# First loads of a gated state-space and feed-forward kernel cut smaller, reordered and spread over other queues

## The chip, the cores and the metric

One core of a Trainium2 chip runs the whole program. The metric is device time in microseconds, the median of several runs. The profile comes from one further execution. Its times start at the beginning of the span that the profile covers.

## The reference

For each of 2048 rows of x (448 wide) the reference mixes two branches with one gate:

```python
g = sigmoid((x * gate_w).sum(-1, keepdims=True))
a = ssm(x)                          # complex linear recurrence over the rows, then a projection, plus x * Dskip
b = silu(x @ w1) @ w2               # w1: 448 x 1792, w2: 1792 x 448
return g * a + (1 - g) * b
```

The recurrence is `h = Lam_bar * h + Bu[t]`, with `Lam_bar = exp(exp(log_dt) * (Lambda_re + 1j * Lambda_im))`. The three vectors `log_dt`, `Lambda_re` and `Lambda_im` (448 values each) are called the parameter rows below.

## The kernel before

**Tiling.** Rows 2k and 2k+1 of x sit side by side, so x is 1024 x 896: the left half holds the even rows, the right half the odd ones. Each half is worked on in two blocks of 512. Matmuls need x transposed (tile XT), with its 448 columns split into blocks j = 0, 1, 2 of 128 and a remainder of 64 (j = 3). W1 (tile W1E) is split in the same way along its rows, and along its 1792 columns into 14 blocks of 128. The columns 0 to 767 (six blocks, `NF1`) are used first.

**Who orders the work.** Every engine's order is written out by hand. A helper (`Tracker`) records each operation with the tiles it reads and writes, and puts a semaphore wait ahead of an operation where one is needed; an engine runs its list strictly in that order. A load is recorded at L226 and a transposing load at L229, whatever tile it fills. Loads issued by SyncE (SP) go to one DMA queue, loads issued by ScalarE (ACT) to another.

**The opening.** TensorE cannot start on data before x and W1 arrive, so it first runs `NWARM` = 20 matmuls on constants (L486). Then, in TensorE's order:

- `turn_k` (L494) transposes 128 x 128 pieces of x on TensorE (L496), k = 0..3 for each j; `turned_x` (L504) lets VectorE (DVE) copy them from PSUM into XT (L507).
- `ffn1_first` (L433) is a generator that issues the 24 matmuls of the first block of rows (L439): for j = 0 twelve of 256 columns (two halves h of the rows times six W1 blocks, `c0` blocks first, then `c1`), for j = 1 and j = 2 six of 512 columns each. It stops at the places listed at L444, and the main program puts other work there.
- `rd` (L470) is a DVE copy inside tile R that needs all three parameter rows; `mm_cols` (L473, matmuls at L477) turns R into columns, and DVE copies them out as PV (L527). PV feeds a chain of small ACT and DVE operations (exp, phases) from L561 on.
- `ffn1_rem` (L448, matmuls at L452) adds the remainder j = 3 to six blocks.
- All later matmuls of the first product and of the input projection go through `lanes` (L366, matmuls at L371).

**The loads before the change** (L287 to L303), each pair on SP and ACT at once: x columns 0 to 127 (two pieces of 64 KB, `ld_x`), W1 rows of j = 0 (two pieces of 96 KB, `ld_w`), x columns 128 to 383 (two of 128 KB), W1 of j = 1 (two of 96 KB, `ld_wh`), the three parameter rows (`ld_row`; two on SP, one on ACT), W1 of j = 2 (two of 96 KB), x columns 384 to 511 (two of 64 KB). Then SP and ACT share the rest of W1: the remainder rows for the first columns (keys W1Er, 48 KB each), columns 768 to 1279 (W1Ed, 256 and 128 KB), the remainder rows for the later columns (W1Es, 64 KB each) and columns 1280 to 1791 (W1Ee, 128 and 256 KB). SP then waits for W1Er (L314) and issues transposing loads of the other rows of x and of B_re and B_im.

**GpSimd (POOL)** meanwhile builds an identity matrix (L330, L331), a ramp IOTA (L334, L336) and a few zeros (L338); it issues no load.

Of the kernel before, what the change touches and what calls it, by code (L numbers as in the profile page):

```python
# [8 lines left out]
AF = mybir.ActivationFunctionType  # L9
# [11 lines left out]
F_FF = 1792  # L21
# [1 line left out]
NK = 1024  # L23
NKT = 8
NF1 = 6
NWARM = 20


class Dma:
# [121 lines left out]
def gated_mix(nc, A_x, A_Lambda_re, A_Lambda_im, A_B_re, A_B_im, A_C_re, A_C_im, A_log_dt,  # L151
              A_Dskip, B_x, B_w1, B_w2, gate_w, out):
    with ExitStack() as ctx:
        E = ctx.enter_context
        T = Tracker(nc, ctx)

        def sb(name, shape, dtype):
            return E(nc.sbuf_tensor(name, list(shape), dtype))
# [5 lines left out]
        W1E = sb("W1E", [128, 4, F_FF], BF16)  # L164
# [16 lines left out]
        JK = sb("JK", [128, 2], BF16)  # L181
# [7 lines left out]
        ID = sb("ID", [128, 128], BF16)  # L189
# [5 lines left out]
        HP = sb("HP", [128, 1], F32)  # L195
# [25 lines left out]
        ps = E(nc.psum_tensor("ps", [128, 8, 512], F32))  # L221
# [3 lines left out]
        def ld(eng, dst, src, key, group=None):  # L225
            return T.dma(eng, lambda e: e.dma_start(dst, src), writes=[key], group=group)  # L226
# [23 lines left out]
        def row(v):  # L250
            return v.rearrange("(o n) -> o n", o=1)

        XH = XN[:, 0:8 * D].rearrange("p (k c) -> p k c", k=4)
        XA = [f"XA{n}{i}" for n in range(3) for i in range(2)]
        FA, FB = 768, 1280
        x0 = x2[0:512, 0:512].rearrange("(k p) c -> p k c", p=128)

        def ld_w(eng, j, f0=0, f1=FA, key=""):
            ld(eng, W1E[:, j, f0:f1], B_w1[j * 128:(j + 1) * 128, f0:f1], f"W1Ej{j}{key}")

        def ld_row(eng, i, v):
            ld(eng, R[i:i + 1, 0:D], row(v), f"R{i}", gR if i < 2 else gR2)

        def ld_w3(eng, j0, j1, f0, f1, key):
            ld(eng, W1E[:, j0:j1, f0:f1], B_w1[j0 * 128:j1 * 128, f0:f1].rearrange("(j p) f -> p j f", p=128),
               f"W1E{key}{j0}")

        def ld_wr(eng, c, later):
            p = slice(64 * c, 64 * c + 64)
            if later:  # L270
                return ld(eng, W1E[p, 3, 384:896].rearrange("p (n f) -> p n f", n=2),
                          B_w1[384:448, FA:].rearrange("p (n c f) -> p n c f", n=2, c=2)[:, :, c, :], f"W1Es{c}")
            return ld(eng, W1E[p, 3, 0:384], B_w1[384:448, 384 * c:384 * c + 384], f"W1Er{c}")

        HALVES = ((0, "sp"), (1, "act"))

        def ld_x(n, c0, c1):
            for i, eng in HALVES:
                k = slice(2 * i, 2 * i + 2)
                ld(eng, XH[:, k, c0:c1], x0[:, k, c0:c1], f"XA{n}{i}")  # L280

        def ld_wh(j):
            for i, eng in HALVES:
                ld(eng, W1E[64 * i:64 * i + 64, j, 0:FA], B_w1[j * 128 + 64 * i:j * 128 + 64 * i + 64, 0:FA],
                   f"W1Ej{j}{i}")

        ld_x(0, 0, 128)  # L287
        for c, eng in HALVES:
            ld_w(eng, 0, 384 * c, 384 * c + 384, c)
        ld_x(1, 128, 384)  # L290
        ld_wh(1)
        for i, (eng, v) in enumerate((("sp", A_log_dt), ("sp", A_Lambda_re), ("act", A_Lambda_im))):
            ld_row(eng, i, v)
        ld_wh(2)
        ld_x(2, 384, 512)
        T.op("act", lambda e: e.activation(JK[:, 0:1], HP[:, :], AF.Exp), reads=["HP"], writes=["JK0"])
        gE = [ld_wr(eng, c, False) for c, eng in enumerate(("sp", "act"))]
        ld_w3("sp", 0, 2, FA, FB, "d")
        ld_w3("act", 2, 3, FA, FB, "d")
        for c, eng in enumerate(("sp", "act")):  # L300
            ld_wr(eng, c, True)
        ld_w3("sp", 0, 1, FB, F_FF, "e")
        ld_w3("act", 1, 3, FB, F_FF, "e")  # L303
        BTK = [f"BT{i}" for i in range(4)] + ["BTz"]
        gBT = T.group()
        def ld_b(dst, src, key):
# [12 lines left out]
        for i, src in enumerate((A_B_re, A_B_im)):  # L319
# [11 lines left out]
        T.op("pool", lambda e: e.affine_select(  # L331
            out=ID[:, :], in_=ID[:, :], pattern=[[-1, 128]], compare_op=ALU.is_equal, fill=0.0,
            base=0, channel_multiplier=1), reads=["ID"], writes=["ID"])
        T.op("pool", lambda e: e.iota(IOTA[:, :].bitcast(I32), pattern=[[1, NK]], base=0, channel_multiplier=0),  # L334
             writes=["IOTA"])
        T.op("pool", lambda e: e.tensor_copy(IOTA[:, :], IOTA[:, :].bitcast(I32)), reads=["IOTA"], writes=["IOTA"])  # L336
# [8 lines left out]
        def nxt():  # L345
            n_bank[0] += 1
            return BANKS[(n_bank[0] - 1) % len(BANKS)]
# [61 lines left out]

        def wj(fb):  # L410
            i, c = fb // 2, fb % 2
            return [f"W1Ej{j}{c}" for j in range(3) for c in range(2)] if i < 3 else ["W1Ed0", "W1Ed2"] if i < 5 else ["W1Ee0", "W1Ee1"]

        def w1(fb):
            return lambda p, j: W1E[p, j, ff(fb) * 128:(ff(fb) + 1) * 128] if j < 3 else \
# [17 lines left out]
        def ffn1_first():  # L433
            banks = [nxt() for _ in range(NF1)]
            for j, h in ((0, 0), (0, 1), (1, None), (2, None)):
                c = slice(0, 512) if h is None else slice(256 * h, 256 * h + 256)
                for n, fb in enumerate((0, 2, 4, 1, 3, 5)):
                    bank = banks[fb]
                    T.op("pe", lambda pe, fb=fb, bank=bank, j=j, h=h, c=c: pe.matmul(  # L439
                        ps[:, bank, c], W1E[:, j, ff(fb) * 128:(ff(fb) + 1) * 128], XT[:, j, c],  # L440
                        start=(h == 0), stop=(h == 0), skip_group_check=(h != 0)),
                        reads=[f"W1Ej{j}{i}" for i in (range(2) if j else (fb % 2,))] + [f"XTe0{j}" if h is None else f"XTe0{j}{h}"],
                        writes=[f"ps{bank}"])
                    if (j, h, n) in ((0, 1, 2), (0, 1, 5), (1, None, 2), (1, None, 5)):  # L444
                        yield
            yield banks

# [34 lines left out]
        def warm(n, b):  # L482
            def mm(pe):
                ins = None
                for _ in range(n):
                    ins = pe.matmul(ps[:, b, 0:128], ones, ones, start=True, stop=True)  # L486
                return ins
            T.op("pe", mm, writes=[f"ps{b}"])

        warm(NWARM, 5)  # L490
        PB = (6, 6, 7, 6)
        xp = [ps[:, b, 0:256].bitcast(BF16) for b in PB]

        def turn_k(j, k, b=None):  # L494
            b = PB[j] if b is None else b
            T.op("pe", lambda pe: pe.transpose(  # L496
                ps[:, b, 0:256].bitcast(BF16)[:, k * 128:(k + 1) * 128], XH[:, k, j * 128:(j + 1) * 128], ID[:, :]),
                reads=[f"XA{(j + 1) // 2}{k // 2}", "ID"], writes=[f"ps{b}"])

        def turn_x(j, i):  # L500
            for k in (2 * i, 2 * i + 1):
                turn_k(j, k)

        def turned_x(j, i=None, b=None):  # L504
            c, key = (slice(0, 512), f"XTe0{j}") if i is None else (slice(256 * i, 256 * i + 256), f"XTe0{j}{i}")
            b = PB[j] if b is None else b
            T.op("dve", lambda e: e.tensor_copy(XT[:, j, c], ps[:, b, 0:256].bitcast(BF16)[:, c]),  # L507
                 reads=[f"ps{b}"], writes=[key])

        for i in range(2):  # L510
            for k in (2 * i, 2 * i + 1):
                turn_k(0, k, 6 + i)
            turned_x(0, i, 6 + i)
        warm(4, 4)
        first = ffn1_first()
        next(first)
        for i in range(2):
            turn_x(1, i)
        turned_x(1)
        next(first)  # L520
        for i in range(2):
            turn_x(2, i)
        turned_x(2)
        rd()
        next(first)
        T.op("pe", mm_cols, reads=["R0", "R1", "R2", "Rd", "ID"], writes=["pv"])
        T.op("dve", lambda e: e.tensor_copy(  # L527
            PV[:, :, :], ps[:, 7, 256:288].rearrange("p (t c) -> p t c", c=8)[:, :, 0:4]),
            reads=["pv", "ps7"], writes=["PV"])
        next(first)  # L530
        for i in range(2):
            turn_x(3, i)

        names = {}

# [5 lines left out]
        def col(n):  # L541
            i = pc(n)
            return P[:, i, :]
# [13 lines left out]
        def pact(o, a, f, ra, scale=1.0, bias=0.0):  # L557
            T.op("act", lambda e: e.activation(col(o), a, f, bias=bias, scale=scale),
                 reads=ra, writes=[o])
# [3 lines left out]
            col("phf"), LIM, 1.0 / TWO_PI, col("dt"), ALU.mult, ALU.mult), reads=["PV", "dt"], writes=["phf"])  # L563
        ptt("ar", col("dt"), LRE, ALU.mult, ["dt", "PV"])
        pact("mag", col("ar"), AF.Exp, ["ar"])
        turned_x(3)
        T.op("dve", lambda e: e.tensor_copy(XR[64:128, 0:512], xp[3][0:64, :]), reads=["ps6"], writes=["XR0a"])
        T.op("act", lambda e: e.activation(JK[:, 0:1], HP[:, :], AF.Silu), reads=["HP"], writes=["JK0"])
        ld_b(GWB, gate_w, "GW")
        ld_b(DB, A_Dskip, "DB")  # L570
        pts("phr", col("phf"), MAGIC, -MAGIC, ALU.add, ALU.add, ["phf"])
# [8 lines left out]
            reads=["f2"] + SGN, writes=["f2s"])  # L580
        first = next(first)
# [54 lines left out]
        def xblock(b):  # L636
            v = XN[:, 4 * b * D:4 * (b + 1) * D].rearrange("p (k c) -> p k c", k=4) if b > 1 else \
                XH[:, :, b * D:(b + 1) * D]
            return v, [*(XA if b < 2 else []), *([f"XN{b // 2}"] if b else [])]

# [24 lines left out]
        for n in (32, 64):  # L665
            T.op("dve", lambda e, n=n: e.tensor_copy(GD[n:2 * n, :, :], GD[0:n, :, :]), reads=["GW", "DB"],
                 writes=["GW", "DB"])
# [7 lines left out]
             writes=["BTz"] + BTK[2:4])  # L675
# [486 lines left out]
        f = ffn1(2)  # L1162
# [100 lines left out]
```

## Time and profile before

| | us |
|---|---|
| median of 3 runs (lowest, highest) | 137.19 (136.63, 137.26) |
| time of the profiled execution | 136.76 |
| its span | 135.2 |
| around the span | 1.56 |
| TensorE busy | 131.8 |
| first matmul on data (L439) | at 4.36 |
| first matmul of `lanes` (L371) | at 10.21 |

The chain of waits lists, in order of time, the pieces of work that led to the last instruction: start, length, what. The timeline lists instructions engine by engine: start, length, engine, line, operation, tile written and tile read, how often. "SPq" and "ACTq" are DMA issues: the length is the time that the issuing queue was held, not the transfer. The view of DMA issues gives KB and the time from issue to landing.

### The profile page before, as it was taken

To read this page: it belongs to the slowest core of one execution; us is meant where nothing else is said; L and a number is where in the kernel's file an instruction comes from. 1 tells how busy PE (TensorE), PEld (TensorE's weight loads), DVE (VectorE), ACT (ScalarE), POOL (GpSimd) and SP (SyncE) were. 2 spreads that over 40 slices of the span, in tenths; PEclk is the share of its full clock that TensorE was granted. 3 is DMA by queue.
4 is the path that set the end of the run, shared out by engine and by line. 5 is a ranking of instruction groups with operands and counts; after the bars stand their busy time and mean duration, and the time that the engine had idled before them with its cause. 6 is when DMAs were issued, how large, how long until landed. Compare 5 with 4: busy or idle time off the path is not lost.

```text
span 135.2 us, 2635 instructions
## 1 busy us (share of the span) xinstructions
PE 131.8 (98%) x1075; PEld 67.3 (50%) x1075; DVE 115.1 (85%) x151; ACT 93.6 (69%) x146; POOL 15.9 (12%) x32
## 2 busy tenths in 40 slices
PE   7899999999999999999999999999999999999993
PEld 7644555554444554444445544445555555555552
DVE  1469999917899798999999999999999999994554
ACT  0459798899939999769999597797114437879200
POOL 7108349550000000000000000000000000000000
PEclk9999999999999999999999999999999999999999
DMA  3889959997996310000222000000000000222123
GB/s 94 244 239 248 184 102 249 175 371 195 263 179 108 70 47 0 0 0 0 60 48 52 5 0 0 0 5 0 0 0 0 0 0 11 95 92 78 68 80 124
DMA packets 25280, 11.78 MB, mean 87 GB/s; under 512 B 17651, under 2 KB 24758, under 8 KB 25270
## 3 DMA queue, kind: packets, MB, share of 16 engines
q1 hardware_dynamic: 23268, 10.47, 32.4%
q10 hardware_dynamic: 2002, 1.17, 3.0%
q8 instruction: 8, 0.13, 0.4%
q14 instruction: 2, 0.02, 0.0%
HBM read 5.34 MB, written 1.84 MB: 53 GB/s over the span
## 4 chain that ended last, share of the span: by engine, by line
PE 95%; DMA 2%; DVE 1%; SPq 0%; issue 0%
PE ps L371 44%; PE ps L795 16%; PE ps L810 16%; PE ps L1048 15%; PE ps L439 3%; DMA W1E<-in_B_w_dram 2%; DVE TMPS L1072 1%; PE ps L496 1%; PE ps L452 1%; SPq L226 0%; PE ps L477 0%
## 5 line engine op out<-in xcount | busy, mean ns | idle before, releaser
L371 PE MATMUL ps<-XT,W1E 64*128 64x512 bf16 x325 | 41.5, 376 | 0.0
L460 ACT ACTIVATE AT<-ps 128x1024 bf16<-128x1024 f32 x28 | 28.2, 1018 | 7.3 <-PE ps L371 7.2
L371 PEld LDWEIGHTS ps<-XT,W1E 64*128 64x128 bf16 x325 | 17.7, 94 | 18.1 <-issue 0.4
L371 PE MATMUL ps<-XT,BT 64*128 64x512 bf16 x156 | 22.5, 376 | 0.0
L810 PE MATMUL ps<-W,AT 64*128 64x448 bf16 x224 | 21.5, 349 | 0.0
L795 PE MATMUL ps<-W,AT 128*128 128x448 bf16 x112 | 21.4, 353 | 0.0
L795 PEld LDWEIGHTS ps<-W,AT 128*128 128x128 bf16 x112 | 10.9, 98 | 10.5 <-issue 0.4
L810 PEld LDWEIGHTS ps<-W,AT 64*128 64x128 bf16 x224 | 10.9, 94 | 10.4
L839 ACT ACTIVATE BT<-ps,GT 128x448 bf16<-128x448 f32 x8 | 5.1, 634 | 13.2 <-PE ps L795 13.2
L895 DVE SCALAR_TENSOR_TENSOR HS<-VE,P,ps 128x512 bf16<-128x512 bf16 (+1 forms) x13 | 9.6, 780 | 3.9 <-PE ps L371 3.9
L371 PEld LDWEIGHTS ps<-XT,BT 64*128 64x128 bf16 x156 | 8.5, 94 | 8.9 <-DVE HS L895 0.3
L939 DVE TENSOR_TENSOR_SCAN G<-P,Q 128x1024 f32<-128x1024 f32 (+1 forms) x6 | 11.4, 1922 | 0.0
L1048 PE MATMUL ps<-CO,VE 128*128 128x448 bf16 (+2 forms) x63 | 11.1, 332 | 0.0
L1048 PE MATMUL ps<-CO,HS 128*128 128x448 bf16 x56 | 11.1, 352 | 0.0
L371 PE MATMUL ps<-XR,W1E 64*128 64x512 bf16 x25 | 9.2, 376 | 0.0
L1048 PEld LDWEIGHTS ps<-CO,VE 128*128 128x128 bf16 x63 | 6.0, 98 | 4.8
L1048 PEld LDWEIGHTS ps<-CO,HS 128*128 128x128 bf16 x56 | 5.5, 98 | 5.1
L892 DVE TENSOR_TENSOR Q<-G,COS 128x2048 bf16<-128x2048 f32 (+1 forms) x4 | 7.0, 1756 | 0.1
L892 DVE TENSOR_TENSOR Q<-G,SIN 128x2048 bf16<-128x2048 f32 (+1 forms) x4 | 7.0, 1751 | 0.0
L857 ACT ACTIVATE VE<-ps 128x1024 bf16<-128x1024 f32 x6 | 6.1, 1020 | 1.2 <-PE ps L371 1.2
L859 ACT ACTIVATE ps<-VE,P 128x1024 f32<-128x1024 bf16 x6 | 6.7, 1118 | 0.2
L895 DVE SCALAR_TENSOR_TENSOR VE<-HS,P,FP 128x512 bf16<-128x512 bf16 (+1 forms) x7 | 6.6, 977 | 0.1
(123 smaller groups left out, 180.7 us busy)
## 6 DMA issues: line engine op xcount, KB each, us to landing
W<-in_B_w_dram SPq DMA_DIRECT2D x2, 784.0 KB, 6.4
XN<-in_A_x_dram SPq DMA_DIRECT2D x1, 896.0 KB, 5.4
out_dram<-OT SPq DMA_DIRECT2D x8, 112.0 KB, 1.7
out_dram<-TMPS SPq DMA_DIRECT2D x7, 112.0 KB, 1.7
HS<-HS SPq DMA_DIRECT2D x4, 128.0 KB, 2.4
XN<-in_A_x_dram SPq DMA_DIRECT2D x1, 384.0 KB, 3.5
W1E<-in_B_w_dram SPq DMA_DIRECT2D x3, 96.0 KB, 3.0
W1E<-in_B_w_dram ACTq DMA_DIRECT2D x3, 96.0 KB, 3.2
```

The lines of the kernel that those rows point to most:

```text
L371: ins = pe.matmul(ps[:, bank, :], w(p, j), xh(odd, h, j, p), start=start and j == js[0], stop=stop and j == js[-1], skip_group_check=seeded)
L439: T.op("pe", lambda pe, fb=fb, bank=bank, j=j, h=h, c=c: pe.matmul(ps[:, bank, c], W1E[:, j, ff(fb) * 128:(ff(fb) + 1) * 128], XT[:, j, c] ...
L460: T.op("act", lambda e: e.activation(a[:, fb:fb + n, :], ps[:, bank:bank + n, :], AF.Silu), reads=[f"ps{bank + i}" for i in range(n)], wri ...
L795: ins = pe.matmul(ps[:, bank, 0:D], a[:, fb, q * 128:(q + 1) * 128], W2[:, ff(fb), :], start=(first and fb == 0), stop=(fb == NFB - 1), sk ...
L810: ins = pe.matmul(ps[:, bank, 0:D], a[p, fb, q * 128:(q + 1) * 128], W2[p, ff(fb), :], start=(start and fb == 0), stop=(not start and fb = ...
L839: T.op("act", lambda e: e.activation(bs(tile), ps[:, bank, 0:D], AF.Copy, scale=sc), reads=[f"ps{bank}", "GT2" if h else "GRI"], writes=ks)
L857: T.op("act", lambda e: e.activation(VE[:, m:m + 2, hs], ps[:, b[0]:b[0] + 2, :], AF.Copy), reads=[f"ps{i}" for i in b], writes=vs)
L859: T.op("act", lambda e: e.activation(ps[:, o[0]:o[0] + 2, :], VE[:, m:m + 2, hs], AF.Copy, scale=c1("lr", pt)), reads=vs + ["lr"], writes= ...
L892: T.op("dve", lambda e: e.tensor_tensor(o, a, b, op), reads=reads, writes=writes)
L895: T.op("dve", lambda e: e.scalar_tensor_tensor(o, a, s, b, ALU.mult, ALU.add), reads=reads, writes=writes)
L939: T.op("dve", lambda e: e.tensor_tensor_scan(G[:, c, w], rb, Q1[:, c, w], init, ALU.mult, ALU.add), reads=[f"Q1{c}", "rr", f"G{c}"], write ...
L1048: ins = pe.matmul(ps[:, bank, c], state(kt, odd, m), CO[:, m, c], start=False, stop=(m == YB[-1]), skip_group_check=True)
```

## The change

- `NWARM` falls from 20 to 16.
- x columns 0 to 127 come in four pieces of 32 KB instead of two of 64 KB, and W1 of j = 0 in four pieces of 48 KB (64 rows by 384 columns) instead of two of 96 KB, in turn.
- x columns 128 to 255 (two of 64 KB) come ahead of W1 of j = 1; x columns 256 to 511 (two of 128 KB) behind it.
- ACT issues only the first seven loads. W1 of j = 2 is one piece of 192 KB on SP, and SP issues all the rest of W1, sixteen loads in all ahead of its first transposing load.
- The three parameter rows are issued by POOL, behind the identity matrix and ahead of IOTA. In the program each is 16 pieces of 28 values; before, each was one piece of 448.
- TensorE's order: the second pair of transposes of j = 0 comes behind the first three matmuls; `mm_cols` comes behind the last matmuls of j = 0 and ahead of those of j = 1 (before: between the two halves of j = 1); the transposes of j = 2 and j = 3 come behind the first and second half of the matmuls of j = 1.
- DVE's order: `rd` and the copy to PV come ahead of the copies of j = 2; the two small operations `phf` and `ar`, which wait for ACT, too.

```diff
-NWARM = 20
+NWARM = 16
...
+        def ld_k(k):
+            for i, eng in HALVES:
+                ld(eng, XH[:, k + i, 0:128], x0[:, k + i, 0:128], f"XA0{k + i}")
+
...
-        def ld_wh(j):
+        def ld_wh(j, f0, f1, key=""):
             for i, eng in HALVES:
-                ld(eng, W1E[64 * i:64 * i + 64, j, 0:FA], B_w1[j * 128 + 64 * i:j * 128 + 64 * i + 64, 0:FA],
-                   f"W1Ej{j}{i}")
-
-        ld_x(0, 0, 128)
-        for c, eng in HALVES:
-            ld_w(eng, 0, 384 * c, 384 * c + 384, c)
-        ld_x(1, 128, 384)
-        ld_wh(1)
-        for i, (eng, v) in enumerate((("sp", A_log_dt), ("sp", A_Lambda_re), ("act", A_Lambda_im))):
-            ld_row(eng, i, v)
-        ld_wh(2)
-        ld_x(2, 384, 512)
+                ld(eng, W1E[64 * i:64 * i + 64, j, f0:f1], B_w1[j * 128 + 64 * i:j * 128 + 64 * i + 64, f0:f1],
+                   f"W1Ej{j}{key}{i}")
+
+        for c in range(2):
+            ld_k(2 * c)
+            ld_wh(0, 384 * c, 384 * c + 384, c)
+        ld_x(1, 128, 256)
+        ld_wh(1, 0, FA)
+        ld_x(2, 256, 512)
         T.op("act", lambda e: e.activation(JK[:, 0:1], HP[:, :], AF.Exp), reads=["HP"], writes=["JK0"])
-        gE = [ld_wr(eng, c, False) for c, eng in enumerate(("sp", "act"))]
+        ld_w("sp", 2)
+        gE = [ld_wr("sp", c, False) for c in range(2)]
...
+        for i, v in enumerate((A_log_dt, A_Lambda_re, A_Lambda_im)):
+            ld_row("pool", i, v)
...
-                    if (j, h, n) in ((0, 1, 2), (0, 1, 5), (1, None, 2), (1, None, 5)):
+                    if (j, h, n) in ((0, 0, 2), (0, 1, 2), (0, 1, 5), (1, None, 2), (1, None, 5)):
                         yield
...
-        for i in range(2):
+        def turn_0(i):
             for k in (2 * i, 2 * i + 1):
                 turn_k(0, k, 6 + i)
             turned_x(0, i, 6 + i)
+
+        def turn_all(j):
+            for i in range(2):
+                turn_x(j, i)
+
+        turn_0(0)
         warm(4, 4)
         first = ffn1_first()
         next(first)
-        for i in range(2):
-            turn_x(1, i)
+        turn_0(1)
+        next(first)
+        turn_all(1)
         turned_x(1)
-        next(first)
-        for i in range(2):
-            turn_x(2, i)
-        turned_x(2)
         rd()
         next(first)
...
-        next(first)
-        for i in range(2):
-            turn_x(3, i)
...
+        next(first)
+        turn_all(2)
+        turned_x(2)
+        next(first)
+        turn_all(3)
         turned_x(3)
```

The remaining W1 loads (`ld_w3`, `ld_wr`) change only from `"act"` to `"sp"`, and the lists of keys follow the new pieces.

More of the change, by code (lines that the diff above doesn't have):

```diff
@@ L253, in gated_mix @@
         XH = XN[:, 0:8 * D].rearrange("p (k c) -> p k c", k=4)
-        XA = [f"XA{n}{i}" for n in range(3) for i in range(2)]
+        XA = [f"XA0{k}" for k in range(4)] + [f"XA{n}{i}" for n in (1, 2) for i in range(2)]
         FA, FB = 768, 1280
@@ L280, in ld_x @@
                 ld(eng, XH[:, k, c0:c1], x0[:, k, c0:c1], f"XA{n}{i}")
-        def ld_wh(j):
+        def ld_wh(j, f0, f1, key=""):
             for i, eng in HALVES:
-                ld(eng, W1E[64 * i:64 * i + 64, j, 0:FA], B_w1[j * 128 + 64 * i:j * 128 + 64 * i + 64, 0:FA],
-                   f"W1Ej{j}{i}")
-        ld_x(0, 0, 128)
-        for c, eng in HALVES:
-            ld_w(eng, 0, 384 * c, 384 * c + 384, c)
-        ld_x(1, 128, 384)
-        ld_wh(1)
-        for i, (eng, v) in enumerate((("sp", A_log_dt), ("sp", A_Lambda_re), ("act", A_Lambda_im))):
-            ld_row(eng, i, v)
-        ld_wh(2)
-        ld_x(2, 384, 512)
+                ld(eng, W1E[64 * i:64 * i + 64, j, f0:f1], B_w1[j * 128 + 64 * i:j * 128 + 64 * i + 64, f0:f1],
[6 more added lines that the diff above has]
+        ld_x(2, 256, 512)
         T.op("act", lambda e: e.activation(JK[:, 0:1], HP[:, :], AF.Exp), reads=["HP"], writes=["JK0"])
-        gE = [ld_wr(eng, c, False) for c, eng in enumerate(("sp", "act"))]
+        ld_w("sp", 2)
+        gE = [ld_wr("sp", c, False) for c in range(2)]
         ld_w3("sp", 0, 2, FA, FB, "d")
-        ld_w3("act", 2, 3, FA, FB, "d")
-        for c, eng in enumerate(("sp", "act")):
-            ld_wr(eng, c, True)
+        ld_w3("sp", 2, 3, FA, FB, "d")
+        for c in range(2):
+            ld_wr("sp", c, True)
         ld_w3("sp", 0, 1, FB, F_FF, "e")
-        ld_w3("act", 1, 3, FB, F_FF, "e")
+        ld_w3("sp", 1, 3, FB, F_FF, "e")
         BTK = [f"BT{i}" for i in range(4)] + ["BTz"]
@@ L411, in wj @@
             i, c = fb // 2, fb % 2
-            return [f"W1Ej{j}{c}" for j in range(3) for c in range(2)] if i < 3 else ["W1Ed0", "W1Ed2"] if i < 5 else ["W1Ee0", "W1Ee1"]
+            return ["W1Ej2"] + [k for h in range(2) for k in (f"W1Ej0{c}{h}", f"W1Ej1{h}")] if i < 3 else ["W1Ed0", "W1Ed2"] if i < 5 else ["W1Ee0", "W1Ee1"]
         def w1(fb):
@@ L441, in ffn1_first @@
                         start=(h == 0), stop=(h == 0), skip_group_check=(h != 0)),
-                        reads=[f"W1Ej{j}{i}" for i in (range(2) if j else (fb % 2,))] + [f"XTe0{j}" if h is None else f"XTe0{j}{h}"],
+                        reads=[f"W1Ej{j}{i}" if j else f"W1Ej0{fb % 2}{i}" for i in (range(2) if j < 2 else ("",))] + [f"XTe0{j}" if h is None else f"XTe0{j}{h}"],
                         writes=[f"ps{bank}"])
-                    if (j, h, n) in ((0, 1, 2), (0, 1, 5), (1, None, 2), (1, None, 5)):
+                    if (j, h, n) in ((0, 0, 2), (0, 1, 2), (0, 1, 5), (1, None, 2), (1, None, 5)):
                         yield
@@ L497, in turn_k @@
                 ps[:, b, 0:256].bitcast(BF16)[:, k * 128:(k + 1) * 128], XH[:, k, j * 128:(j + 1) * 128], ID[:, :]),
-                reads=[f"XA{(j + 1) // 2}{k // 2}", "ID"], writes=[f"ps{b}"])
+                reads=[f"XA{min(j, 2)}{k // 2}" if j else f"XA0{k}", "ID"], writes=[f"ps{b}"])
         def turn_x(j, i):
@@ L565, in gated_mix @@
         pact("mag", col("ar"), AF.Exp, ["ar"])
+        T.op("act", lambda e: e.activation(JK[:, 0:1], HP[:, :], AF.Silu), reads=["HP"], writes=["JK0"])
+        next(first)
[3 more added lines that the diff above has]
+        turn_all(3)
         turned_x(3)
         T.op("dve", lambda e: e.tensor_copy(XR[64:128, 0:512], xp[3][0:64, :]), reads=["ps6"], writes=["XR0a"])
-        T.op("act", lambda e: e.activation(JK[:, 0:1], HP[:, :], AF.Silu), reads=["HP"], writes=["JK0"])
         ld_b(GWB, gate_w, "GW")
```

## The prediction

> **What bounds the kernel now.** I read the chain of waits first: it tells whether TensorE ever waits once it has started.
>
> ```profile
> 1.31 3.01 DMA W1E<-in_B_w_dram
> ...
> 4.36 1.16 PE ps L439 x9
> ...
> 6.35 0.81 PE ps L439 x3
> ...
> 9.62 0.75 PE ps L452 x6
> 10.37 31.86 PE ps L371 x294
> ```
>
> The chain starts with one load, the first W1 piece, issued at 1.31 and landed 3.01 us later. From 4.36 on it is TensorE without a break. The 294 matmuls from 10.37 on take 31.86 us, 108 ns each, with no wait between them; the chain goes on so up to the last output (the page gives it 95% TensorE). So the change can act only ahead of L371, whose first matmul starts at 10.21 in the timeline. I call that start the handover. What it gains there the end gains, unless a later load or copy then comes too late.
>
> Next the timeline of the opening.
>
> ```profile
> 0.82 2.29 PE L486 MATMUL ps<-const-bfloat16-1.0 128*128 128x128 bf16 x20 [0.82 <-PEq L1248]
> 1.06 0.29 POOL L331 TENSOR_SCALAR_AFFINE_SELECT ID<-ID 128x128 bf16<-128x128 bf16 x1
> 2.93 0.91 ACTq L226 DMA_DIRECT2D R<-in_A_Lambda_im_dram  x1
> 3.43 0.31 SPq L226 DMA_DIRECT2D R<-in_A_Lambda_re_dram  x1
> 4.36 1.16 PE L439 MATMUL ps<-XT,W1E 128*128 128x256 bf16 x9 [0.38 <-DMA W1E<-in_B_w_dram]
> 5.36 0.39 PE L496 MATMUL ps<-ID,XN 128*128 128x128 bf16 x4
> 5.78 0.97 DVE L507 COPY XT<-ps 128x512 bf16<-128x512 bf16 x2 [1.83 <-PE ps L496]
> 6.35 0.81 PE L439 MATMUL ps<-XT,W1E 128*128 128x512 bf16 x3
> 6.67 0.16 DVE L471 COPY R<-R 3x64 bf16<-3x64 bf16 x1
> 7.00 0.24 PE L477 MATMUL ps<-ID,R 128*128 128x4 bf16 x4
> 8.35 3.11 SPq L229 DMA_TRANSPOSE XT<-in_A_x_dram  x2
> 10.41 1.74 POOL L608 TENSOR_SCALAR FP<-IOTA,P 128x1024 f32<-128x1024 f32 x1 [6.22 <-DVE P L555]
> ```
>
> TensorE's start at 4.36 is a wait for W1, but what follows is already tied to DVE: the first matmul of j = 1 starts at 6.35, only when the first of DVE's two copies (0.97/2 = 0.48 us, from 5.78) has ended. From 6.35 to the handover there are 3.86 us. Work in them: 12 matmuls of 512 columns at 0.215 us apart (6.35, 6.57, 6.78) make 2.58, four transposes at 0.055 make 0.22, `mm_cols` 0.10 (7.00 to 7.10), three pairs of L452 0.66 (9.55 to 10.21): 3.56 in all. Only 0.3 us is idle (0.2 before the second pair of j = 3 transposes, 0.1 before L452).
>
> Last, how long loads take, by window: KB, then microseconds from issue to landing.
>
> ```profile
> XN<-in_A_x_dram SPq DMA_DIRECT2D x1, 64.0 KB, 2.2
> W1E<-in_B_w_dram SPq DMA_DIRECT2D x1, 96.0 KB, 3.0
> XN<-in_A_x_dram SPq DMA_DIRECT2D x1, 128.0 KB, 3.2
> XN<-in_A_x_dram ACTq DMA_DIRECT2D x1, 128.0 KB, 3.4
> ```
>
> The first load, with nothing ahead of it, lands after 2.2 us; with a full queue ahead it takes 3.0 to 3.4. Issues follow each other by about 0.5 us per queue (0.78, 1.31, 1.81, 2.28).
>
> **The change, part by part.**
>
> *Smaller first pieces.* The seven pairs are now issued at about 0.8, 1.3, 1.8, 2.3, 2.8, 3.3 and 3.9. Ahead of the first matmul stand 64 KB of x and 96 KB of W1, where it was 128 and 192. Each landing is bounded by the rows 2.2 and 3.4. I take 2.3 for the first four, as half as much is queued and the nearest row is the unloaded 2.2: W1 `c0` at 3.6 (now 4.32), the second x pair at 4.1, W1 `c1` at 4.6. So TensorE starts 0.75 us earlier, but then stands still for `c1`: the early start alone is worth nothing, as it stops at 4.6.
>
> *x columns 128 to 255 ahead of W1 of j = 1.* Issued at 2.8 and taken at 2.4: landed at 5.2 (the larger piece landed at 5.0 and 5.25). TensorE gets there after `c1`: six matmuls of 256 columns at 0.11 us, 4.6 + 0.66 = 5.26; four transposes, 0.22: 5.48. DVE's copy begins 0.20 after the transposes (5.58, then 5.78), 0.48 long: 6.16. `rd` follows, 0.16: 6.32. `mm_cols` came 0.17 after `rd` (6.83, then 7.00): now about 6.45. W1 of j = 1, issued at 3.3 and taken at 2.6, is there at 5.9 and hidden.
>
> *`mm_cols` ahead of j = 1.* From 6.45 stands all that is left: `mm_cols` 0.10, the 12 matmuls 2.58, now eight transposes 0.44 (those of j = 2 stood ahead of 6.35 before, in a gap), L452 0.66: 3.78, handover at 10.23. The new loads hold this up little: x columns 256 to 511 (issued 3.9, 3.0: 6.9) are wanted at 6.45 + 0.10 + 0.65 = 7.20, W1 of j = 2 (issued 4.4, 3.2: 7.6) at 8.3, W1Er (issued 4.9 and 5.4, 3.0: 8.4) at 9.6. DVE's copy of j = 2 stands behind `phf` and `ar`; those ended 1.1 us after the start of PV's copy (7.28 to 8.37), and `mm_cols` to PV took 0.28, so the copy could start at 6.45 + 0.28 + 1.1 = 7.8 and end at 8.3, about when j = 2 starts. Sum for this path: 10.23 against 10.21, **nothing**. If every first load needs only 2.0 us, the `c1` wait ends 0.3 earlier and so does all: -0.3. If they need the loaded 3.4, `c1` lands at 5.7: +1.1.
>
> *Parameter rows from POOL.* No row shows a load issued by POOL. POOL is free at 1.35 (end of L331). Three issues: at the cheapest like SP's row, 0.31 each, the last starting at 2.0 and landing 2.2 later at 4.2; at the dearest like a transposing load on SP (3.11/2 = 1.55 each), the last starting at 4.45 and landing 3.4 later at 7.85. I take the 0.91 of ACT's row, the nearest in kind: last issue at 3.2, landing 2.8 later (between 2.2 and 3.4): 6.0, just inside the 6.16 at which `rd` wants it. Cost nothing, with little cover. [...] POOL's IOTA, zeros and the rest move back by 0.9 to 4.6 us; they ended at 4.2 and L608 needs them at 10.41, so they stay hidden. SP and ACT lose three issues (0.31 to 0.91) between W1 of j = 1 and j = 2; that is in the issue times above.
>
> *SP alone for the rest of W1.* SP issues sixteen loads instead of twelve. After eight (to about 4.9) come eight at 0.61 (four took 2.45): its transposing loads start at about 9.8 instead of 8.35. All loads that follow land about 1.4 us later. What covers it: the other rows of XT landed at about 13.4 and are used from 16.2; the B loads landed by 19.75 and DVE's copy of them ran at 20.52 without waiting, then TensorE needs that copy at 23.0; it may come 2 us later. W1Ed (issued 6.0 and 6.6, 3.5 later: 9.5 and 10.1) is wanted at 10.2, W1Es (by 7.8 + 2.8 = 10.6) at 10.9, W1Ee (by 9.1 + 3.5 = 12.6) at 13.2. Close, and nothing if the queue moves as before. ACT, freed of seven issues, has nothing to do earlier with: its first Silu waits for L452.
>
> *Four warm-up matmuls less*: 4 x 0.107 = 0.43 us, in time that waits for x anyway.
>
> **Sum.** 10.23 - 10.21, about 0: 136.76 for the profiled execution. That one lay 0.43 below the median of the runs. I forecast **137.1**, the median less a trifle for landings that may be quicker than taken. (0.5%, 0.69 us, is about what a measurement of this kernel can tell from no change.)
>
> **Rivals.**
>
> - *POOL's rows come late.* `mm_cols` stands on TensorE ahead of all of j = 1, and `rd` on DVE ahead of PV and the copies of j = 2 and 3, so every tenth of a microsecond past 6.16 goes into the end. At the dearest, 7.85: +1.7; halfway, 6.9: +0.75, 137.9. For it: three issues stand in a row on an engine whose small operations are slow (L331 0.29 us; L704, 128 x 4, 1.05 us at 24.73). Against: each row has only 0.9 KB. It decides from 6.9 on for a measurable loss. Chance 0.22.
> - *The early start is kept whole.* If DVE and the loads keep up, the handover moves by the 0.75 us of the first matmul: 136.4. Against it: the copy that held 6.35 stands in the new order too. Chance 0.13.
> - *TensorE stays slow at the start.* The warm-up matmuls follow each other by 107 ns, transposes at 5.36 by 55; the change of pace falls between 3.98 and 4.36, after 3.2 to 3.5 us of nearly unbroken work. Now the work has holes (2.5 to 2.9, and before `c1`). If the pace stays halved until 8, the matmuls from 5.3 to 8 lose about 1.4 us: 138.6. [...] Against: the holes are short. Chance 0.07.
> - *W1's later columns come late*, as one queue has what two had: TensorE waits at 10.2 to 10.9 for W1Ed or W1Es, +0.3 to +0.8 (137.4 to 138.0). Chance 0.10.
>
> The forecast has 0.48. Faster: the second rival less a part that stays below 0.69, 0.13. Slower: most of the first (0.17), the third and half of the fourth: 0.29. The rest, 0.58, is within 0.5%. The range leaves out the dear end of POOL's price and takes the others in: 136.4 to 138.2.
>
> **What would show it.** First L439 at about 3.6, a hole on TensorE until about 4.6; `mm_cols` near 6.45 with the idle time before it ended by DVE; first L371 near 10.2; POOL's three issues ended by 4.2. Idle time of DVE's L471 or of L477 ended by a load of R shows the first rival; matmuls of 256 columns 0.21 apart after 4.4 the third; idle time at the first L371 ended by W1E the fourth. It is wrong if the handover is before 9.6 or after 10.9, or if TensorE waits after it.

## The result and the profile after

The changed kernel is slower: 138.63 us median of 6 runs (138.28 to 139.17) against 136.75 (136.61 to 137.26) for the kernel before on the same chip, a ratio of 1.0133 (95% interval 1.0103 to 1.0163). The forecast was 137.1 with a range up to 138.2. The profiled execution took 138.74, its span 137.3 (before: 136.76 and 135.2); what lies around the span is about the same (1.44 against 1.56).

L443 of the changed kernel is L439 of before (first matmuls), L500 is L496 (transposes), L481 is L477 (`mm_cols`), L456 is L452, L375 is L371 (`lanes`), L511 and L475 are the DVE copies L507 and L471. The chain of waits of the changed kernel (start, length, what):

```profile
0.78 0.39 SPq L226
...
1.24 0.56 SPq L226
...
1.85 0.82 SPq L226
...
2.71 2.62 DMA W1E<-in_B_w_dram
...
5.38 1.46 PE ps L443 x6
6.85 0.43 PE ps L500 x4
...
7.96 0.25 PE ps L481 x4
8.21 1.04 PE ps L443 x3
9.25 0.22 PE ps L500 x4
...
11.64 0.76 PE ps L456 x6
12.39 31.92 PE ps L375 x294
```

Before, one issue stood in the chain ahead of the W1 transfer issued at 1.31. Now the chain begins with three issues on SP, one after the other, and only the fourth, at 2.71, is the `c1` piece of W1 that TensorE waits for until 5.38. The last line is the same work as before in the same time (31.92 against 31.86). So the loss lies ahead of the handover: in the timeline, the first L375 starts at 12.23, where it was 10.21, 2.02 us later; the span is 2.1 longer.

The chain also shows TensorE at half pace. Six matmuls of 256 columns take 1.46 (they start 0.213 apart); nine of them took 1.16 before (0.11 apart). Four transposes take 0.43 at 6.85 and 0.22 at 9.25. The pace doubles in between, at 8.8.

The timeline of the same opening:

```profile
1.85 0.82 SPq L226 DMA_DIRECT2D XN<-in_A_x_dram  x1
...
2.72 0.48 POOL L226 DMA_DIRECT2D R<-in_A_Lambda_im_dram  x1
...
3.74 0.82 PE L443 MATMUL ps<-XT,W1E 128*128 128x256 bf16 x3 [0.26 <-DMA W1E<-in_B_w_dram]
...
5.06 5.23 SPq L226 DMA_DIRECT2D W1E<-in_B_w_dram  x9
...
5.38 1.46 PE L443 MATMUL ps<-XT,W1E 128*128 128x256 bf16 x6 [0.59 <-DMA W1E<-in_B_w_dram]
...
7.31 0.42 DVE L511 COPY XT<-ps 128x512 bf16<-128x512 bf16 x1 [2.19 <-PE ps L500]
7.65 0.16 DVE L475 COPY R<-R 3x64 bf16<-3x64 bf16 x1
...
10.40 3.44 SPq L229 DMA_TRANSPOSE XT<-in_A_x_dram  x2
...
12.23 1.18 PE L375 MATMUL ps<-XT,W1E 64*128 64x512 bf16 x7
```

The last row is the handover. In the kernel before it was

```profile
10.21 1.12 PE L371 MATMUL ps<-XT,W1E 64*128 64x512 bf16 x7
```

TensorE starts early as planned (3.74), then stands idle for 0.59 us until `c1` lands. DVE's copies no longer set anything: they follow TensorE's transposes. POOL's rows are issued by 3.2.

The view of DMA issues (KB, us from issue to landing), window 0 to 11:

```profile
XN<-in_A_x_dram SPq DMA_DIRECT2D x1, 128.0 KB, 4.0
...
W1E<-in_B_w_dram SPq DMA_DIRECT2D x1, 96.0 KB, 3.7
...
XN<-in_A_x_dram SPq DMA_DIRECT2D x1, 64.0 KB, 2.8
...
R<-in_A_Lambda_im_dram POOLq DMA_DIRECT2D x1, 0.9 KB, 2.1
```

With the issue times this puts x columns 128 to 255 at 6.0, W1 of j = 1 (issued at 3.88) at 7.58 and x columns 256 to 511 (issued at 4.40) at 8.4. The prediction had 5.2, 5.9 and 6.9. The rows were there by 4.8.

One row of the view by windows says how this happened. Its last columns are TensorE's granted clock, the mean busy share of the DMA engines and GB/s. Before:

```profile
2.00:5.00 3.00, 2.62 (x25) 2.15 (x23) 0.51 (x2) 0.00 (x0) 1.89 (x6) 1.00 0.92 251
```

After:

```profile
2.00:5.00 3.00, 2.53 (x18) 1.39 (x15) 0.46 (x2) 0.25 (x1) 2.92 (x5) 1.00 0.60 129
```

From 2 to 5 us half as much arrives. An issue held SP for 0.43 to 0.57 us before, with 64 to 128 KB in it. It now holds SP for 0.39 to 0.82 us with 32 or 48 KB in it. Meanwhile the DMA engines are busy for 0.60 of the stretch, where it was 0.92: the queues, not the transfers, set the rate. The granted clock reads 1.00 in both rows, though matmuls of 256 columns are 0.213 apart in the second; in the opening the pace has to be read from the spacing.

These views don't tell what each cause is worth: the late pieces, TensorE's half pace (which may follow from them), POOL's rows, and SP alone for the later loads. The experiments take these apart. The kernel before ran beside each batch (136.75 to 137.03 us), and the ratios are to those runs. Two of e2's four runs, with a mean granted clock of 0.976 where every other run has 1.0, are left out of its ratio.

### The profile page after: what moved, and what is told of

Its sections match the earlier page's. It is cut to its first block, busy times and chain, and to the rows that moved or that the text cites. A ratio compares the mean times of both kernels' runs of the same rounds, so it can differ in the third digit from the quotient of the medians.

```text
span 137.3 us, 2633 instructions
## 1 busy us (share of the span) xinstructions
PE 133.5 (97%) x1071; PEld 67.5 (49%) x1071; DVE 115.3 (84%) x151; ACT 93.7 (68%) x146; POOL 17.5 (13%) x35
## 3 DMA queue, kind: packets, MB, share of 16 engines
HBM read 5.34 MB, written 1.84 MB: 52 GB/s over the span
## 4 chain that ended last, share of the span: by engine, by line
PE 94%; DMA 2%; SPq 1%; DVE 1%; issue 0%
PE ps L375 43%; PE ps L804 16%; PE ps L819 15%; PE ps L1057 15%; PE ps L443 4%; DMA W1E<-in_B_w_dram 2%; SPq L226 1%; DVE TMPS L1081 1%; PE ps L500 1%; PE ps L456 1%; PE ps L481 0%
## 5 line engine op out<-in xcount | busy, mean ns | idle before, releaser
L375 PE MATMUL ps<-XT,W1E 64*128 64x512 bf16 x325 | 41.5, 376 | 0.0
L375 PEld LDWEIGHTS ps<-XT,W1E 64*128 64x128 bf16 x325 | 17.8, 94 | 18.2 <-issue 0.5
L375 PE MATMUL ps<-XT,BT 64*128 64x512 bf16 x156 | 22.5, 376 | 0.0
L375 PEld LDWEIGHTS ps<-XT,BT 64*128 64x128 bf16 x156 | 8.5, 94 | 8.8 <-DVE HS L904 0.3
L375 PE MATMUL ps<-XR,W1E 64*128 64x512 bf16 x25 | 9.3, 376 | 0.0
L443 PE MATMUL ps<-XT,W1E 128*128 128x256 bf16 (+1 forms) x24 | 6.6, 414 | 0.9 <-DMA W1E<-in_B_w_dram 0.9
L511 DVE COPY XT<-ps 128x512 bf16<-128x512 bf16 (+1 forms) x5 | 1.9, 371 | 6.2 <-PE ps L500 6.2
```

The costliest lines, as they stand in the source:

```text
L375: ins = pe.matmul(ps[:, bank, :], w(p, j), xh(odd, h, j, p), start=start and j == js[0], stop=stop and j == js[-1], skip_group_check=seeded)
```

## The experiments

**e1: holes of TensorE filled.** The changed kernel, with

```diff
-        warm(4, 4)
+        warm(8, 4)
...
         turn_0(1)
+        warm(10, 5)
         next(first)
```

> The changed kernel with TensorE's holes filled by more matmuls on constants: eight instead of four behind the first two transposes, and ten more ahead of the wait for the second W1 piece (c1). Loads and all other orders as in the changed kernel. Theory A (half pace): in the changed kernel the pace of TensorE doubles only at 8.87 us, as the holes keep it slow, and that costs 6 x 0.105 + 4 x 0.053 + 0.36 = 1.2 us of the 2.0; here the pace doubles near 4.3, matmuls of 256 columns from c1 on follow each other by 0.11 us, the handover (first matmul of lanes) moves from 12.23 to about 11.0 and the time falls by about 1.2 us. Theory B (late loads alone make the loss, as TensorE waits for them at either pace): the time stays within 0.3 us of the changed kernel.

Measured: 138.52, ratio 1.0119 (1.0091 to 1.0147); 0.1 us gained, which the intervals cannot tell from nothing. The pace doubled at 6.9 instead of 8.8, but ten extra matmuls ran past the landing of `c1` (first `c1` matmul at 5.79), and `mm_cols` came at 8.04. The chain shows what then ended last:

```profile
8.60 4.20 DMA W1E<-in_B_w_dram
...
12.93 31.28 PE ps L375 x288
```

TensorE reached `lanes` at 11.95 and soon waited for a W1Es piece that SP had issued only at 8.60. A faster TensorE meets loads that are late too.

**e2: rows later on POOL.** The changed kernel, with the three row loads behind IOTA and its cast.

```diff
-        for i, v in enumerate((A_log_dt, A_Lambda_re, A_Lambda_im)):
-            ld_row("pool", i, v)
         T.op("pool", lambda e: e.iota(...))
         T.op("pool", lambda e: e.tensor_copy(IOTA...))
+        for i, v in enumerate((A_log_dt, A_Lambda_re, A_Lambda_im)):
+            ld_row("pool", i, v)
```

> The changed kernel with the three parameter rows issued by POOL behind IOTA and its conversion, at about 3.5 us instead of 1.49, so that none of POOL's issues falls between SP's third and fourth issue. Theory C (POOL's issues hold up SP's): SP's third issue falls from 0.82 to about 0.5 us, W1 c1 is issued at 2.35 instead of 2.71 and lands 0.35 earlier, and the time falls by about 0.35 us. Theory D (small pieces of x are simply slow to issue): the third issue stays above 0.6 us and the time stays within 0.2 us. By both the rows land by about 7.3, ahead of the 7.65 at which DVE takes them.

Measured: SP's third issue still held its queue for 0.82 us, so POOL's loads are not what slows it. The time is a miss of mine: 141.5 (139.13 to 141.99), and a ratio of 1.0239 (1.0155 to 1.0323) by the two shorter runs, 139.13 and 141.05. Issued at 4.71 behind full queues, the last row took 3.78 us instead of 2.1, and `mm_cols` came at 8.89: the first rival's mechanism, which the change itself escaped. Its profile, of a run of 141.94, also showed the pace going back. The view by windows (TensorE busy is the first pair after the comma, its granted clock the third column from the end):

```profile
4.70:8.10 3.40, 1.56 (x16) 1.02 (x13) 0.72 (x2) 1.49 (x2) 0.95 (x6) 1.00 0.88 243
8.10:11.50 3.40, 2.39 (x12) 1.29 (x14) 1.01 (x5) 1.71 (x4) 0.00 (x0) 0.50 0.80 214
11.50:14.90 3.40, 3.40 (x12) 1.33 (x10) 2.08 (x12) 0.19 (x1) 0.22 (x1) 0.50 1.05 213
14.90:18.30 3.40, 3.40 (x33) 1.41 (x34) 3.30 (x4) 2.83 (x5) 3.14 (x3) 1.00 0.87 163
```

The pace had doubled at 4.7. In the next 3.4 us TensorE was busy for only 1.56, and it went back to half for 6.8 us, twice 3.4; only after a stretch of 3.4 us that was all busy did it double again. These 6.8 us at half pace account for all that its mean clock of 0.976 lacks; the two shorter runs have 1.0.

**e3: later loads shared.** The changed kernel, with ACT issuing its half of the later W1 loads again.

```diff
-        ld_w("sp", 2)
-        gE = [ld_wr("sp", c, False) for c in range(2)]
+        ld_wh(2, 0, FA)
+        gE = [ld_wr(eng, c, False) for c, eng in enumerate(("sp", "act"))]
...
-        ld_w3("sp", 2, 3, FA, FB, "d")
+        ld_w3("act", 2, 3, FA, FB, "d")
...
-        ld_w3("sp", 1, 3, FB, F_FF, "e")
+        ld_w3("act", 1, 3, FB, F_FF, "e")
```

> The changed kernel with ACT issuing its half of the later W1 loads again (W1 of j = 2 in two halves, W1Er, W1Ed, W1Es and W1Ee split as before the change); the opening loads, POOL's rows and all engine orders stay. If SP alone costs nothing, as the prediction had it, the time stays within 0.3 us, while SP's transposing loads start at about 8.5 instead of 10.40. If the later loads hold TensorE up anywhere, the time falls by 0.3 to 0.8 us.

Measured: 138.48, ratio 1.0122 (1.0101 to 1.0142). The matmuls of `c1` began at 5.34 (5.38 in the changed kernel), SP's transposing loads at 9.59 instead of 10.40. The single queue is not the cause of the 1.9 us.

**e4: sixteen warm-ups in the kernel before** (`NWARM = 16`, nothing else).

> The kernel before with 16 instead of 20 matmuls on constants ahead of the first transposes, and nothing else changed. If the four matmuls less are what keeps the pace halved (a hole of 0.45 us from 2.5 to 3.0), matmuls of 256 columns follow each other by 0.21 us from 4.36 on and the time grows by 0.8 to 1.3 us. If it takes the longer holes behind them, the pace doubles before 4.36 as in the kernel before and the time stays within 0.3 us.

Measured: 137.33, ratio 1.0038 (1.0015 to 1.0062), with a wider spread (136.8 to 138.41). So four warm-ups less are not free, though the prediction had them so.

**e5: e1 and e3 together, with six extra matmuls instead of ten.**

> The changed kernel with both undone at once: TensorE's holes filled (eight constants matmuls behind the first transposes, six ahead of c1, where ten overran the landing of c1 by 0.4 us before), and ACT issuing its half of the later W1 loads again. Theory E (two limits one behind the other): the changed kernel's half pace and its last W1 piece for the first pairs of lanes (W1Es, issued by SP at 8.57, landed at 12.87, wanted at 12.88) end at the same place, so undoing one alone gave under 0.2 us, and undoing both gives more: the handover at 11.2 to 11.6 without a wait for W1E behind it, 0.6 to 1.0 us under the changed kernel, 137.6 to 138.0. Theory F (only the late c1 counts): as each alone, 138.4 to 138.6.

Measured: 138.52, ratio 1.0106 (1.007 to 1.014). In its profile (137.91) the pace doubled at 5.3 and nothing waited after the handover, yet the handover came at 11.52. The matmuls of j = 1 could begin only at about 7.6, when their W1 rows landed (issued at 3.88; the trace lacks the first of these matmuls and has the second at 7.85). Half pace is thus not the whole loss: late loads alone hold the handover 1.3 us back.

**e6: large first pieces.** The changed kernel, with the first x and W1 pieces at their old sizes; everything else as changed.

```diff
-        for c in range(2):
-            ld_k(2 * c)
-            ld_wh(0, 384 * c, 384 * c + 384, c)
+        for i, eng in HALVES:
+            T.dma(eng, ... XH[:, 2 * i:2 * i + 2, 0:128] ...)
+        for c, eng in HALVES:
+            T.dma(eng, ... W1E[:, 0, 384 * c:384 * c + 384] ...)
```

> The changed kernel with only the first pieces made large again (x columns 0 to 127 in two pieces of 64 KB, W1 of j = 0 in two of 96 KB, c0 on SP and c1 on ACT at once); order of the rest, POOL's rows, SP alone for the later W1 loads and all engine orders stay. Theory G (four issues in a row ahead of c1 are what makes it late): c0 lands near 4.3 instead of 3.7 but c1 near 4.5 instead of 5.33, every later load is issued about 1.3 us earlier (W1Es near 7.4, landed near 11.6), TensorE gets from c1 on 0.8 us earlier, and the time falls by 0.8 to 1.2 us, to about 137.6. Theory H (half pace alone is the loss): it stays within 0.4 us of the changed kernel, as the pace stays halved just as long.

Measured: 137.63, ratio 1.0048 (1.0022 to 1.0074). One microsecond of the 1.9 is gone by the sizes alone. The window from 2 to 5 us:

```profile
2.00:5.00 3.00, 2.65 (x20) 1.89 (x18) 0.39 (x2) 1.23 (x1) 2.92 (x5) 1.00 0.89 222
```

Nearly the old rate (222 GB/s; 251 before, 129 after), and the chain has no W1 wait left (L446, L503 and L378 are L443, L500 and L375 of the changed kernel):

```profile
3.85 0.80 PE ps L446 x3
4.65 0.21 PE ps L503 x2
4.86 1.28 PE ps L446 x6
...
11.14 31.76 PE ps L378 x294
```

**e7: e6 with the later loads shared (e3) and 20 warm-ups.**

> As the last kernel (large first pieces), with ACT issuing its half of the later W1 loads again and 20 constants matmuls at the start. What is left of the change is then: x columns 128 to 255 ahead of W1 of j = 1, the rows on POOL, and the new orders on TensorE and DVE. If the small first pieces, SP alone and the half pace are the whole loss, the time is that of the kernel before or a little less (136.4 to 136.9); if the new order with the parameter columns ahead of j = 1 costs something by itself, 137.1 to 137.6.

Measured: 137.31, ratio 1.0018 (1.0002 to 1.0033). `mm_cols` ran at 6.54 in its profile; the prediction had 6.45 for the full change. There TensorE had waited 0.36 us, and DVE's `rd` ended the wait, as predicted. The handover still came at 10.51, 0.28 later than forecast.

**e8: the kernel before, with only the rows moved to POOL.**

> The kernel before with one thing changed: the three parameter rows issued by POOL behind the identity matrix. SP and ACT lose 0.9 us of issues between W1 of j = 1 and j = 2; the rows land at about 4.8. Expected: x columns 384 to 511 land 0.5 to 0.9 earlier, the 0.2 us that TensorE waits for them goes, and the time falls by 0.1 to 0.3 us. Rival: a third queue costs the others something, and the time grows by 0.2 us or more.

Measured: 136.72 against 137.03, ratio 0.9979 (0.9960 to 0.9998). This one part of the change may even gain about 0.2%; it is the best version found.

**e9: the kernel before, with only the first pieces made small.**

```diff
-        ld_x(0, 0, 128)
-        for c, eng in HALVES:
-            ld_w(eng, 0, 384 * c, 384 * c + 384, c)
+        for c in range(2):
+            for i, eng in HALVES:
+                ld(eng, XH[:, 2 * c + i, 0:128], x0[:, 2 * c + i, 0:128], f"XA0{2 * c + i}")
+            for i, eng in HALVES:
+                ld(eng, W1E[64 * i:64 * i + 64, 0, 384 * c:384 * c + 384], ...)
```

> The kernel before, with one part of the change alone: x columns 0 to 127 in four pieces of 32 KB and W1 of j = 0 in four of 48 KB, in turn. If the small first pieces are the main cause (each issue holds its queue for 0.4 to 0.8 us whatever its size, so two more issues per queue delay every later load by about 1.1 us), the second W1 piece lands near 5.3, the x columns 128 to 383 near 6.3, the handover comes 0.8 to 1.2 us later and the time is about 137.8 (ratio 1.006 to 1.010). If the loss comes from small pieces only together with the new order of TensorE and the single queue, the time stays within 0.3 us of the kernel before.

Measured: 138.94, ratio 1.0161 (1.0133 to 1.0190): 2.1 us, twice what I expected, and as much as the whole change. Two rows of its timeline (L499 is L496) and one by window:

```profile
1.86 0.82 SPq L226 DMA_DIRECT2D XN<-in_A_x_dram  x1
...
4.88 0.39 PE L499 MATMUL ps<-ID,XN 128*128 128x128 bf16 x2 [1.56 <-DMA XN<-in_A_x_dram]
```

```profile
2.00:5.00 3.00, 1.44 (x15) 1.18 (x13) 0.29 (x1) 0.00 (x0) 1.90 (x6) 1.00 0.65 147
```

The third issue takes 0.82 us here too, with no load on POOL. In the old order all four transposes of j = 0 stand ahead of the first matmul, so TensorE stands still for 1.56 us, until the second x pair has landed. The changed order, which lets three matmuls go first, has holes of 0.26 and 0.59 us instead.

**e10: the changed kernel with 20 warm-ups.**

> The changed kernel with 20 warm-up matmuls instead of 16. If four warm-ups less are what keeps TensorE at half pace until 8.9, the pace now doubles before 5.5, the handover comes at 11.2 to 11.6 and the time is 0.5 to 0.8 us below the changed kernel (about 137.9). If the late loads set the time by themselves (the filled holes and the shared late loads brought 0.1 us), it stays above 138.3.

Measured: 138.96, ratio 1.0140 (1.0097 to 1.0182); pace doubled at 10.2, handover at 12.93. Four warm-ups more don't help while `c1` is late.

**e11 and e12: second profiles of the kernel before and of the changed kernel.**

> The kernel before, unchanged, with a second profile. If the moment at which TensorE's pace doubles (between 3.98 and 4.36 in the first profile) belongs to the kernel's order of work, it is there again within 0.2 us. If it is a matter of the single run (a window whose phase is free), it comes elsewhere, up to about 6.1, and the handover moves by half of the delay times the share of TensorE that is busy, at most 0.5 us.

> The changed kernel, unchanged, with a second profile. If half pace until 8.87 belongs to the kernel, it is there again, with the handover near 12.2. If it is a matter of the single run, the pace doubles earlier (between 4.5 and 8) and the handover comes at 11.4 to 12.0, since W1 of j = 1 and j = 2 land at 7.6 and 8.9 either way.

Measured: the kernel before doubled its pace at 3.9 again (3.8 in the first profile), and took 137.21, since an x piece for j = 3 took 4.16 us and the handover was at 10.75. The changed kernel stayed at half pace even longer than in its first profile, until 11.9. Its chain:

```profile
2.73 2.91 DMA W1E<-in_B_w_dram
...
5.69 1.46 PE ps L443 x6
...
8.51 1.32 PE ps L443 x3
...
14.03 31.76 PE ps L375 x294
```

Three matmuls of 512 columns take 1.32 at 8.51, where the first profile had 1.04. Handover 13.87, time 140.26. Both expectations for it were wrong: the pace neither repeats nor comes earlier.

**e13 and e14: e6 with 20 warm-ups, and e6 with the later loads shared.**

> The changed kernel with large first pieces (x columns 0 to 127 in two of 64 KB, W1 of j = 0 in two of 96 KB) and 20 warm-up matmuls; SP still issues all the later loads of W1 alone. With large pieces alone the ratio was 1.0048, with 20 warm-ups and shared later loads as well 1.0018. If the four warm-ups are what is left, this gives about 1.002. If the single queue is what is left, it stays near 1.005, with transposing loads of SP near 8.9.

> The changed kernel with large first pieces and ScalarE issuing its half of the later loads of W1, as before the change; 16 warm-up matmuls. If the single queue is what is left after the large pieces, the ratio is about 1.002. If the four warm-ups are, it stays near 1.005: TensorE then has a hole of 0.3 us at 2.7, and its pace doubles near 6 instead of 4.5 where the window of 3.4 us falls so.

Measured: 137.39, ratio 1.0028 (1.0010 to 1.0047), and 137.35, ratio 1.0019 (0.9998 to 1.0040). Each seems to take a part of e6's 0.48%, but the three intervals overlap: how the rest is divided stays open.

## Why the prediction was wrong

**The cause.** Ratios to the kernel before:

| | first pieces large | first pieces small |
|---|---|---|
| old order, queues and warm-ups | 1 | 1.0161 (e9) |
| new order, queues and warm-ups | 1.0048 (e6) | 1.0133 (the change) |

Small first pieces cost 2.1 us in the old order and 1.0 to 1.2 in the new one. They alone, without the rest of the change, are as slow as the whole of it. The other parts together cost 0.5% with large pieces, of which the warm-ups and the single queue seem to make most (e7: 0.18% left, but its interval overlaps that of e6). Pieces of x and of W1 were made small together in every run; which of them costs more stays open.

**The step that failed** is "I take 2.3 for the first four, as half as much is queued", with the issue times in front of it. Both terms were mis-sized, because I took the queue to be filled with bytes, while it is filled with issues: they followed each other by 0.60 us on average instead of about 0.5, and W1 of j = 1, fourth in its queue before (at 2.28) and sixth now, was issued at 3.88 and took 3.70, where the prediction had 3.3 and 2.6. A second step failed with it: "six matmuls of 256 columns at 0.11 us" took the pace as doubled by then, and they ran 0.213 apart. Against the path of the prediction, from the chain and the timeline of the changed kernel:

| term | predicted | measured | difference |
|---|---|---|---|
| `c1` there, first of six matmuls | 4.60 | 5.38 | +0.78 |
| six matmuls, four transposes | 0.88 | 1.89 | +1.01 |
| from there to `mm_cols` | 0.97 | 0.69 | -0.28 |
| `mm_cols` and the first three of j = 1 | 0.75 | 1.29 | +0.54 |
| the rest up to the handover | 3.03 | 2.98 | -0.05 |
| handover | 10.23 | 12.23 | +2.00 |

The first row is the landing: issued at 2.71 instead of 2.3, as the third issue took 0.82, and 2.62 long instead of 2.3. The second and fourth (1.55 together) are mostly half pace: 0.62 for the six matmuls, 0.21 for the transposes and 0.39 for the first three of j = 1, 1.2 in all. They can't be had back alone: W1 of j = 1 at 7.58 and 3.68 us of work behind it put the handover at 11.3 at the earliest, 1.1 after the old one, and e5, with the pace early, measured 11.52. The prediction's own bound for loaded landings was +1.1; I put the value at the other end, by the row of a load with nothing ahead of it.

**Why the pace doubles so late.** The prediction named this as the third rival, priced it at +1.4 and gave it 0.07, "the holes are short". Its mechanism came true. That its 138.6 is so close to what came is in part luck, as it has no late landing in it, while half pace cost 1.2 and not 1.4. Sixteen profiles, ordered by the time at which the spacing of matmuls halves (holes are idle stretches of TensorE ahead of that):

| profile | holes | pace doubles | handover | its time |
|---|---|---|---|---|
| before, again (e11) | none; none | 3.8; 3.9 | 10.21; 10.75 | 136.76; 137.21 |
| e7, e13, e5 | none; 0.12; 0.13 | 4.5; 4.9; 5.3 | 10.51; 10.71; 11.52 | 136.63; 137.63; 137.91 |
| e6, e4, e8, e14 | 0.30; 0.27; none; 0.34 and 0.16 | 6.0; 6.1; 6.2; 6.6 | 10.97; 10.56; 10.59; 11.33 | 137.56; 136.95; 136.74; 137.43 |
| e1 | none | 6.9 | 11.95 | 138.69 |
| e3 | 0.25 and 0.43 | 7.2 | 11.82 | 138.21 |
| e9 | 1.56 | 7.9 | 12.31 | 138.89 |
| after, e10, again (e12) | 0.26 and 0.59; 0.13 and 0.60; 0.30 and 0.81 | 8.8; 10.2; 11.9 | 12.23; 12.93; 13.87 | 138.74; 139.18; 140.26 |
| e2 | 0.37 | 4.7, halved at 8.1, doubled at 14.9 | 15.69 | 141.94 |

(A gap of 0.22 in e10 at 8.80 and one in e12 at 10.25 are matmuls that the trace lacks, no holes.) What fits all sixteen, as my reading of them, is a window of 3.41 us that runs on by itself: the pace doubles at the end of the first window that holds less than about half a microsecond of idle time. The length is in the traces: the record of the granted clock reads 1.0 for 133.12 us in the kernel before and for 129.71 in the changed kernel, 3.41 apart, 39 and 38 such lengths; in e2 the rows by window show full pace for 3.4 and half pace for 6.8. In the first two the record begins at the very times of the table (3.78 before, 8.84 after). Without a long hole, work starts at 0.82, and the pace doubles between 3.8 and 6.9, by where the window happens to lie. The wait for `c1` (0.59 to 0.81 us in the profiles of after, e10 and e12) spoils each window that it falls in; work then starts anew at 5.4 to 5.7, and the pace doubles 3.5 to 6.2 later. In e3 it was 0.43 and did not. So the same late piece costs its 0.78 us and then, by this reading, a further window. That the window runs on by itself and the half microsecond were not tested by themselves: of the windows after which the pace doubled, e3's had the most idle time, 0.48, and of those after which it did not, one of e12 had the least, about 0.5.

**The other steps.**

- *TensorE starts at 3.6, then stands still for `c1`*: right (3.74, then 0.59 idle); the hole was longer and later than taken.
- *`mm_cols` near 6.45, its wait ended by DVE*: 7.96 in the change, 6.54 in e7. The order of work was read rightly, for pieces that land in time.
- *Parameter rows from POOL, nothing, with little cover*: right in time, with more cover than thought. Issues took 0.74, 0.49 and 0.48 instead of 0.91, landings 2.1 to 2.4 us: there by 4.8 instead of 6.0. In other runs landings took longer: 2.7 to 3.4 us in e6, and 3.78 for the last row in e2, behind full queues. The first rival had 0.22 and did not happen.
- *Four warm-ups less, nothing*: wrong by 0.4% in e4. That "time that waits for x anyway" is also time in which the window counts would explain it, but is not shown: in e4's profile (136.95) the pace doubled at 6.1, but in e8's, which has all its warm-ups and no hole, at 6.2.
- *SP alone, close and nothing*: SP's transposing loads came at 10.40 (predicted 9.8). W1Es landed at 12.89, just when a late TensorE wanted it. e1 shows that it is the next limit: 12.80, and TensorE waits.
- *After the handover nothing changes*: right (31.92 against 31.86).
- *The early start kept whole* did not happen; the *later columns late* show only where TensorE is faster (e1).

## What to carry to other kernels

At the start of a kernel count issues, not bytes: as long as each load holds its queue for 0.4 to 0.8 us whatever its size (here 32 to 128 KB), halving the first pieces halves the rate at which everything behind them arrives (here from 251 to 129 GB/s between 2 and 5 us), and only what stands first comes sooner (here the first matmul on data at 3.74, where it was 4.36). A start that is earlier and then waits can be worse than a later one without a hole, as the hole can keep TensorE at half pace for longer (here it was 0.6 us, and the pace doubled only 3.5 us after it). Try each part of such a change alone: here one part of it (rows on POOL) was harmless or a small gain, and another (small first pieces) by itself made a loss as large as the whole.

## What the runs showed of the hardware that was not expected

- A load of 32 KB, one 128-row piece of x, held SP's queue for 0.39 to 0.40 us as the first issue and for 0.81 to 0.83 as the third, in every profile with small pieces; loads of 64 to 128 KB among the first seven of SP took 0.43 to 0.64. Why the third is dear stays open (not POOL's loads: e2, e9). Here the issues set the rate (DMA engines busy for 0.60 of the stretch from 2 to 5 us, 0.92 before).
- In e2 a hole of 2.08 us on TensorE, with one of 0.54 ahead of it, was followed by half pace for 6.8 us: of the 3.40 us ahead of that, 1.84 were idle.
- The view's granted clock reads 1.00 in the opening, whatever the pace, as the trace's record of the clock begins only where the pace doubles (3.78 in the kernel before, 8.84 in the changed kernel); the spacing of equal matmuls (0.213 or 0.109 us at 256 columns) tells the pace.
